# Gated scan with two MLPs: weight signs and sums on GpSimd, no plain group in the second unit, a first slot of native fp32 products

## The chip, the cores and the metric

One core of one Trainium2 chip runs the whole program. The metric is the device time of one execution in microseconds (us). The kernel before takes 1967.82 us, the median of three runs (1967.82 to 1968.0).

## The reference, cut to what matters

```python
sig = 1 / (1 + exp(-f_logit));  f = lb + (1 - lb) * sig;  i = 1 - f
h = 0
for t in range(6080):                # 2 batches, 256 features
    h = f[:, t] * h + i[:, t] * x[:, t];  y[:, t] = h
x1 = square(max(y @ w_in1, 0)) @ w_out1          # 12160 tokens, 256 -> 2048 -> 256
h2 = x1 @ w_in2
out = where(h2 > 0, h2, exp(min(h2, 0)) - 1) @ w_out2     # 256 -> 2048 -> 256
```

All is fp32. A gated recurrence along the sequence is followed by two MLPs over 12160 tokens.

## The kernel before, in words

**Arithmetic.** TensorE multiplies fp32r operands. Each fp32 operand is split into a rounded high part (a copy with fp32r output, mostly on ScalarE) and a low part (the operand minus its high part, on VectorE). `three` (L894) forms one product by three matmuls: high·high, high·low, low·high. GpSimd takes hardly any part.

**Units and slots.** The tokens are cut into units of two halves; the first unit has halves of 512 and 384 tokens, the others of 512 and 512 (the end differs). The 2048 inner features are cut into 8 groups. The work on one group of one unit is a slot. In a *plain* slot of one half, two feature blocks k times two outputs make four products, 12 matmuls. In a *mixed* slot both halves are combined by sums and differences of operands, so that seven products (21 matmuls) stand for the eight of two plain slots (24 matmuls). Mixed slots need four sums of each weight tile (`weight_sums`, L378 to L382) and differences of the features (`minus`, L611). `plain` (L248) says which slots are plain: all of the first layer's first unit, and with `PLAIN_G = 1` also group 0 of the second unit. Then `add_mixed_parts` and `add_later_parts` make that unit's operands; a unit without plain slots is served by `add_parts`.

**Weights.** `add_weights` (L424) makes each of the 32 weight tiles once. SP loads the raw tile (`st`); ScalarE takes the scaled magnitude of the high words (L437) and converts the low words (L440); VectorE shifts and joins them (`magnitude`, L443), then sets the sign bit (`sign`, L446); ScalarE makes the high part (L474) and VectorE the low part (L480). First-layer input tiles are kept in DRAM and loaded again for later units.

**The first unit.** x and f_logit rows come in four chunks (256, 256, 256, 128 tokens). For each, TensorE transposes the rows (L739), ScalarE takes a tanh (L746, L770), a gate is formed (L795/L797; for the chunks after the first by GpSimd), VectorE multiplies (L753, L776) and scans (L818). The scan runs on features not yet multiplied by `ga = 0.5 - 0.5·lb`; `split_scaled` (L549) multiplies while it makes the high part (ScalarE, L551) and the low part (VectorE, L554). For the first half, `add_first_parts` (L558) does that per chunk and feature block, four pairs in all. `products_of` (L1042) issues the first slot as two sets of 12 matmuls of 256 columns. Spins (L716) are transposes of a constant ahead of the real work.

**Order.** TensorE's order of products is written out by `pe_order`, with due times. All other steps are given to `Order`, a planner with a cost, a due time, reads and writes for each step; it decides the order on each engine, and for some steps between ScalarE and VectorE. Each engine then runs its list in order. SP issues nearly all DMAs: rows, weights, copies kept in DRAM, reloads, spills, results. `EARLY` and `WDUE` place the first weight loads and weight steps, `LOADS` names the first-unit slots before which the second unit's row loads may not start, `FIRST_DUE` the first split parts.

Of the kernel before, what the change touches and what calls it, by code (L numbers as in the profile page):

```python
# [11 lines left out]
U32 = mybir.dt.uint32  # L12
AF = mybir.ActivationFunctionType
# [3 lines left out]
P = 128  # L17
# [4 lines left out]
PLAIN_G = 1  # L22
# [4 lines left out]
GAP = 56  # L27
TURN = 0.125
# [3 lines left out]
EARLY = (-18.5,)  # L32
DUE1 = 3.0
FIRST_SLOTS = True
SPIN = (11, 16, 5)
C_DUE = 1.0
# [4 lines left out]
WDUE = (-6.0, -4.0, -2.0, 0.0)  # L41
FIRST_DUE = (-10.0, -6.0)
# [7 lines left out]
LOADS = (6, 8, 10, 12)  # L50
# [20 lines left out]
class Order:  # L71
# [47 lines left out]
    def run(self):  # L119
# [33 lines left out]
        while any(ready.values()):  # L153
            best = None
            for e, r in ready.items():
                if not r:
                    continue
                t0 = max(free[e], min(r.values()))
                n = min((n for n, t in r.items() if t <= t0 + self.HOLD), key=lambda n: steps[n][2])
                if t0 < self.RAMP:  # L160
                    late = t0 > self.CALM
                    v = min((n for n, t in r.items() if t <= t0 + self.WAIT[late]), key=lambda n: steps[n][2])
                    if steps[v][2] < steps[n][2] - self.FAR[late]:
# [28 lines left out]
def kernel(  # L192
# [67 lines left out]
    def slots_of(m, u):  # L260

        if not plain(m, u):
            return [(m, u, None, g) for g in range(KG)]
        a, b = ([(m, u, h, g) for g in range(KG) if plain(m, u, g)] for h in range(2))
        if u == 0 and FIRST_SLOTS:
            got, a, b = [*a[:3], *b[:1]], a[3:], b[1:]
            return got + [s for pair in zip(b, a) for s in pair] + b[-2:]
# [110 lines left out]
    def weight_sums(q, a):  # L378
        nc.vector.tensor_tensor(q[:, 0], a[:, 0], a[:, 2], op=ALU.add)
        nc.vector.tensor_tensor(q[:, 2], a[:, 1], a[:, 0], op=ALU.subtract)  # L380
        nc.vector.tensor_tensor(q[:, 1], q[:, 0], a[:, 1], op=ALU.subtract)
        nc.vector.tensor_tensor(q[:, 3], a[:, 3], q[:, 1], op=ALU.subtract)  # L382
# [41 lines left out]
    def add_weights(i, m, kind, c, due, wk=None):  # L424
# [22 lines left out]

        def sums(e):
# [53 lines left out]
        w = wk if kind == 0 else ("w", m, c)  # L502
        over = [("raw", k) for k in range(KG) if m == kind == 1]
# [3 lines left out]
            ["DVE", dve(CE), low_part, [a], [w]],  # L507
# [4 lines left out]
    def add_sums(c, due):  # L512
# [8 lines left out]
        chain(due - 4.0, [["DVE", 4 * dve(P), sums, [("raw", c)], [q]]])  # L521
# [12 lines left out]

    F_t = {}
# [22 lines left out]
    def add_first_parts(F, k, src, dst, due):  # L558

        x_k[0, 0, 0] = [(*k, q, c, p) for q in range(2) for c in range(KD) for p in range(2)]  # L560
        for q, (at, n) in enumerate(chunks(0, 0)):
            for c in range(KD):
                high, low = split_scaled(c, lambda at=at, n=n, c=c: src()[:, c, at : at + n], lambda at=at, n=n, c=c: dst()[:, :, c, at : at + n])
                hi, lo = (*k, q, c, 0), (*k, q, c, 1)
                order.add("ACT", act(n), due + FIRST_DUE[q] - 1.0 + C_DUE * c, high, [(*F[q], c)] + [(*k, 0, 0, 0)] * (q + c > 0), [hi])
                order.add("DVE", dve(n), due + FIRST_DUE[q] + C_DUE * c, low, [hi, (*F[q], c)], [lo])

# [152 lines left out]
    def add_scan(i, u, h, q, due, after=None, from_=None):  # L720
# [58 lines left out]
        def load_bound(e):  # L779
            nc.scalar.dma_start(lb, lower_bound.rearrange("(i c) -> i c", c=KD))  # L780

# [17 lines left out]

        def bound(e):  # L800
            nc.vector.tensor_scalar(ga, lb, -0.5, 0.5, op0=ALU.mult, op1=ALU.add)
            nc.vector.tensor_scalar(gb, lb, 0.5, 0.5, op0=ALU.mult, op1=ALU.add)
# [36 lines left out]
        if u == 0:  # L839
# [5 lines left out]
            if i == 0:  # L845
                order.add("ACT", 0.6, -30.0, load_bound, (), [("lb",)], None, 1)
            if i == 0:
                add_spin(SPIN[0], due - 7.0)
            if i == 0 and BY_TILE:
# [5 lines left out]
                order.add("DVE", 0.2, -2.0, bound, [("lb",)], [("bound",)])  # L855
# [10 lines left out]
            if i == 1:  # L866
# [3 lines left out]
                *([["DVE", 0.2, bound, [("lb",)], [("bound",)]]] if i == 0 else []),  # L870
                *(["POOL", 0.05 + n / 256, gate(c), [("bound",), fT] + [(*gT, 0)] * c, [(*gT, c)]] for c in range(KD)),
# [145 lines left out]
    def add_plain(s, wk):  # L1017
# [24 lines left out]
        def products_of(q):  # L1042
            def go(e):
                at, m = chunks(u, h)[q]
                for w, k, c in PLAIN_PRODUCTS:
# [3 lines left out]
                    three(t[c][:, cols], ws_t[wk], w, x_t[0, u, h][:, :, :, cols], k, k == 0, k == 1, True)  # L1049
# [200 lines left out]

    weights = []
# [21 lines left out]
    for due, what, m, g, who in weights:  # L1273
# [12 lines left out]
        else:  # L1286
            add_weights(n_prep, m, int(what == "out"), g, due + WDUE[min(n_prep, len(WDUE) - 1)], wk)
# [85 lines left out]
```

## Time and profile before

| | us |
|---|---|
| median of three runs | 1967.82 |
| time of the profiled execution | 1967.67 |
| its span | 1965.9 |
| TensorE busy (matmul) | 1957.9 |
| VectorE busy | 1504.6 |
| ScalarE busy | 1624.9 |
| GpSimd busy | 7.9 (12 instructions) |

The profiled execution lies 0.15 us below the median, and 1.8 us of its time lie outside the span. The granted clock is full over the whole span. Busy shares are means over stages that have different limits: the start, the first unit (about 80 us), the long middle, and the end.

### The profile page before, as it was taken

Reading aid. Unit: us, or ns where it says so; the run is one execution under the profiler, and the core shown is the slowest. Engines: PE = TensorE matmul, PEld = TensorE weight load, DVE = VectorE, ACT = ScalarE, POOL = GpSimd, SP = SyncE. Lnnn points to the kernel's source line nnn. Section 1 sums busy time; section 2 is a strip of 40 time slices with the busy share of each in tenths; the row PEclk is TensorE's granted clock in tenths of the full one; section 3 lists DMA queues with packets and bytes.
Section 4 is the critical chain, followed back from the end, with each engine's and each line's share of the span. In section 5 each row is a group of like instructions: output and inputs, shape, how many; then the busy total and the mean of one; then the engine's idle time right before and its main releaser. Section 6 shows DMA issues by size and latency. Waiting matters only on the chain.

```text
span 1965.9 us, 23805 instructions
## 1 busy us (share of the span) xinstructions
PE 1957.9 (100%) x8739; PEld 1634.4 (83%) x8739; DVE 1504.6 (77%) x1938; ACT 1624.9 (83%) x2184; POOL 7.9 (0%) x12
## 2 busy tenths in 40 slices
PE   9999999999999999999999999999999999999999
PEld 8888888888888888888888888888888888888888
DVE  8998889877776876877777687687775668778686
ACT  8989899888788878888878887887887878878786
POOL 1000000000000000000000000000000000000000
PEclk9999999999999999999999999999999999999999
DMA  7775565532533433354243343324323324242332
GB/s 255 222 234 191 193 190 191 179 128 85 147 126 115 130 106 134 105 148 137 86 137 136 105 137 115 122 101 127 136 94 107 122 99 137 94 136 97 114 116 74
DMA packets 226564, 265.80 MB, mean 135 GB/s; under 512 B 151696, under 2 KB 154256, under 8 KB 226448
## 3 DMA queue, kind: packets, MB, share of 16 engines
q1 hardware_dynamic: 224448, 263.83, 41.6%
q8 instruction: 68, 1.11, 0.2%
q10 hardware_dynamic: 2000, 0.46, 0.1%
q14 instruction: 48, 0.39, 0.1%
HBM read 222.56 MB, written 41.68 MB: 134 GB/s over the span
## 4 chain that ended last, share of the span: by engine, by line
PE 99%; DVE 1%; ACT 0%; issue 0%; POOL 0%; DVEq 0%; POOLq 0%
PE a L1181 53%; PE c L896 46%; DVE F L818 0%; PE a L716 0%; DVE wo L443 0%; PE c L739 0%; DVE wo L446 0%; DVE xT L776 0%; DVE o L1220 0%; DVE F L480 0%; ACT st L440 0%; DVE ws L480 0%; ACT wo L437 0%; ACT xa L551 0%; DVE xT L753 0%
## 5 line engine op out<-in xcount | busy, mean ns | idle before, releaser
L1181 PE MATMUL a<-g,wo 128*128 128x512 f32 (+2 forms) x4608 | 1156.3, 387 | 0.0
L1181 PEld LDWEIGHTS a<-g,wo 128*128 128x128 f32 x4608 | 863.8, 188 | 171.3
L1117 ACT ACTIVATE r<-c 128x512 f32<-128x512 f32 (+1 forms) x732 | 427.1, 583 | 252.6 <-PE c L896 246.1
L944 DVE TENSOR_TENSOR g<-r,g 128x1024 fp32r<-128x1024 f32 (+2 forms) x382 | 461.6, 1208 | 139.8 <-ACT g L939 131.4
L1124 DVE TENSOR_TENSOR r<-c,r 128x512 f32<-128x512 f32 (+1 forms) x549 | 375.5, 684 | 193.4 <-PE c L896 189.7
L939 ACT ACTIVATE g<-r 128x1024 fp32r<-128x1024 f32 (+2 forms) x382 | 401.7, 1052 | 68.5 <-PE a L1181 51.8
L896 PE MATMUL c<-xa,ws 128*128 128x512 f32 (+2 forms) x1719 | 446.2, 387 | 1.0 <-DVE ws L480 0.9
L896 PEld LDWEIGHTS c<-xa,ws 128*128 128x128 f32 x1719 | 321.2, 188 | 65.7 <-DVE ws L480 1.1
L896 PE MATMUL c<-xb,ws 128*128 128x512 f32 (+2 forms) x1152 | 318.0, 386 | 0.0
L934 DVE SCALAR_TENSOR_TENSOR r<-e,r 128x1024 f32<-128x1024 f32 (+1 forms) x190 | 230.7, 1214 | 105.0 <-ACT e L931 105.0
L896 PE MATMUL c<-xc,ws 128*128 128x512 f32 (+1 forms) x1104 | 308.9, 388 | 0.0
L896 PEld LDWEIGHTS c<-xb,ws 128*128 128x128 f32 x1152 | 215.7, 188 | 42.2
L896 PEld LDWEIGHTS c<-xc,ws 128*128 128x128 f32 x1104 | 207.1, 188 | 42.1
L931 ACT ACTIVATE e<-e 128x1024 f32<-128x1024 f32 (+1 forms) x190 | 198.8, 1046 | 0.7
L928 ACT ACTIVATE e<-r 128x1024 f32<-128x1024 f32 (+1 forms) x190 | 197.0, 1041 | 0.4
L922 ACT ACTIVATE r<-r 128x1024 f32<-128x1024 f32 (+1 forms) x186 | 194.1, 1044 | 0.2
L915 ACT ACTIVATE r<-r 128x1024 f32<-128x1024 f32 x87 | 91.2, 1048 | 0.0
L614 DVE TENSOR_TENSOR F<-F 128x512 f32<-128x512 f32 (+1 forms) x92 | 62.8, 683 | 1.0
L918 ACT ACTIVATE r<-r 128x512 f32<-128x512 f32 x87 | 53.7, 617 | 0.0
L818 DVE TENSOR_TENSOR_SCAN F<-fT,F,xT 128x256 f32<-128x256 f32 x66 | 48.2, 742 | 0.7
L545 DVE TENSOR_TENSOR xa<-F,xa 128x512 fp32r<-128x512 f32 (+3 forms) x47 | 43.6, 932 | 0.4
L1220 DVE STREAM_TRANSPOSE o<-a 128x512 f32<-128x512 f32 (+1 forms) x48 | 31.2, 686 | 1.2 <-PE a L1181 1.2
(89 smaller groups left out, 621.6 us busy)
## 6 DMA issues: line engine op xcount, KB each, us to landing
ws<-wd SPq DMA_DIRECT2D x183, 896.0 KB, 4.8
xd<-o SPq DMA_DIRECT2D x46, 256.0 KB, 2.9
fs<-in_f_logit_dram SPq DMA_DIRECT2D x176, 64.0 KB, 2.3
xs<-in_x_dram SPq DMA_DIRECT2D x176, 64.0 KB, 2.5
F<-xd SPq DMA_DIRECT2D x22, 512.0 KB, 4.4
out_dram<-o SPq DMA_DIRECT2D x88, 128.0 KB, 5.3
st<-in_moe_w_in_dram SPq DMA_DIRECT2D x16, 512.0 KB, 4.6
st<-in_moe_w_out_dram SPq DMA_DIRECT2D x16, 512.0 KB, 4.7
```

The costliest lines, as they stand in the source:

```text
L614: nc.vector.tensor_tensor(f[:, to], f[:, i], f[:, k], op=ALU.subtract)
L896: nc.tensor.matmul(out, lhsT=ws[:, p, w], rhs=xs[:, r, v], start=start and q == 0, stop=stop and q == 2, skip_group_check=check,)
L915: nc.scalar.activation(r_t[0], r_t[0], AF.Relu)
L922: nc.scalar.activation(r_t[0], r_t[0], AF.Square)
L928: nc.scalar.activation(t["e"], r_t[0], AF.Relu, scale=-1.0)
L931: nc.scalar.activation(t["e"], t["e"], AF.Exp, scale=-1.0)
L934: nc.vector.scalar_tensor_tensor(r_t[0], t["e"], 1.0, r_t[0], op0=ALU.subtract, op1=ALU.max)
L939: nc.scalar.activation(g_t[s, which][:, 0], r_t[0], AF.Copy)
L944: nc.vector.tensor_tensor(g_t[s, which][:, 1], r_t[0], g_t[s, which][:, 0].bitcast(F32), op=ALU.subtract)
L1117: nc.scalar.activation(r[0][:, i], t[A], f)
L1124: nc.vector.tensor_tensor(r[:, i], t[tag], r[:, i], op=ALU.add)
L1181: nc.tensor.matmul(a, lhsT=y, rhs=v, start=begin and jj == 0 and p == 0, stop=end and jj == len(mine) - 1 and p == 2, skip_group_check=True,)
```

## The change

- `weight_sums` is issued on GpSimd in place of VectorE.
- For weight tiles from the fifth on (`BYTES = 4`), VectorE's `sign` is left out. GpSimd writes a byte of 0 or 128 (`sign_byte`) into the top byte of the converted low word, between the conversion and `magnitude`, which then joins the sign too.
- `PLAIN_G = 0`: the second unit has only mixed slots and uses `add_parts`.
- The first slot multiplies unsplit features by `first["w"]`, the first tile times `ga` (ScalarE, `times_ga`), with native fp32 matmuls: 8 of 256 columns for 24 fp32r ones. The first tile's split comes `W_LATER` later, its low part on GpSimd. The first half's features are split over all 512 tokens at once, two pairs in place of four.
- The second chunk's gate for feature block 0 goes from GpSimd to VectorE or ScalarE.
- The second weight tile's load is put early on SP (`EARLY`), due times of the second and third tile move, the second unit's row loads may start after slots 2, 4, 6, 8, and the planner's holding rules differ before 22 us of its own clock. Load and use of the lower bound move in the source, with the same due times.

```diff
-PLAIN_G = 1
+PLAIN_G = 0
+UNTIL = 22.0
+HOLD0 = 0.1
+FAR0 = 5.0
+BYTES = 4
+SIGN_US = 1.8
-EARLY = (-18.5,)
+EARLY = (-18.5, -16.5)
-WDUE = (-6.0, -4.0, -2.0, 0.0)
-FIRST_DUE = (-10.0, -6.0)
+WDUE = (-6.0, -7.0, -5.0, 0.0)
+ADUE = -2.0
+W_LATER = 6.0
+RAW_MM = 1.78
-LOADS = (6, 8, 10, 12)
+LOADS = (2, 4, 6, 8)
...
     def weight_sums(q, a):
-        nc.vector.tensor_tensor(q[:, 0], a[:, 0], a[:, 2], op=ALU.add)
+        nc.gpsimd.tensor_tensor(q[:, 0], a[:, 0], a[:, 2], op=ALU.add)
...
+        def sign_byte(e):
+            b = t["st"].bitcast(U8).rearrange("p k e w -> p (k e) w")[:, :, 3]
+            nc.gpsimd.tensor_scalar(b, t["high"].bitcast(F32), 0.0, 128.0, op0=ALU.is_lt, op1=ALU.mult)
...
         def low_part(e):
             for v, hi, lo in parts():
-                nc.vector.tensor_tensor(lo, v, hi.bitcast(F32), op=ALU.subtract)
+                (nc.gpsimd if e == "POOL" else nc.vector).tensor_tensor(lo, v, hi.bitcast(F32), op=ALU.subtract)
...
+        if i >= BYTES:
+            steps[3:] = [["POOL", SIGN_US, sign_byte, [], [st]], ["DVE", dve(CE), magnitude, [st], [a]]]
...
-            chain(due - 6.0, [*steps, ["DVE", 4 * dve(P), sums, [a], [q]]])
+            chain(due - 6.0, [*steps, ["POOL", 2.5, sums, [a], [q]]])
...
+        if i == 0:
+            def times_ga(e):
+                first["w"] = new("a", [P, 4, P])
+                for k in range(KD):
+                    nc.scalar.activation(first["w"][:, 2 * k : 2 * k + 2], t["a"][:, 2 * k : 2 * k + 2], AF.Copy, scale=ga[:, k : k + 1])
+
+            first["key"] = key_of("a")
+            chain(due, [*steps, ["ACT", act(CE) + 0.1, times_ga, [a, ("bound",)], [first["key"]]]])
+            steps = []
+            due += W_LATER
...
-            ["DVE", dve(CE), low_part, [a], [w]],
+            ["POOL", 2.0, low_part, [a], [w]] if i == 0 else ["DVE", dve(CE), low_part, [a], [w]],
...
-        chain(due - 4.0, [["DVE", 4 * dve(P), sums, [("raw", c)], [q]]])
+        chain(due - 4.0, [["POOL", 2.5, sums, [("raw", c)], [q]]])
...
-        x_k[0, 0, 0] = [(*k, q, c, p) for q in range(2) for c in range(KD) for p in range(2)]
-        for q, (at, n) in enumerate(chunks(0, 0)):
-            for c in range(KD):
...
+        n = units[0][0]
+        x_k[0, 0, 0] = [(*k, c, p) for c in range(KD) for p in range(2)]
+        for c in range(KD):
+            high, low = split_scaled(c, lambda c=c: src()[:, c], lambda c=c: dst()[:, :, c])
...
-                *(["POOL", 0.05 + n / 256, gate(c), [("bound",), fT] + [(*gT, 0)] * c, [(*gT, c)]] for c in range(KD)),
+                *(["POOL", 0.05 + n / 256, gate(c), [("bound",), fT] + [(*gT, 0)] * c, [(*gT, c)]] if i > 1 or c else ["DVE", dve(n) + 0.08, gate(c), [("bound",), fT], [(*gT, c)], ("ACT", act(n) + 0.24)] for c in range(KD)),
...
-                    three(t[c][:, cols], ws_t[wk], w, x_t[0, u, h][:, :, :, cols], k, k == 0, k == 1, True)
+                    nc.tensor.matmul(
+                        t[c][:, cols], lhsT=first["w"][:, w], rhs=F_t[0, u][:, h + 2 * k, cols],
+                        start=k == 0, stop=k == 1, skip_group_check=True,
+                    )
...
-                x_k1 = x_k[m, u, h][4 * q : 4 * q + 4]
-                n1 = order.add("PE", COLD[q] * 6 * ROW * n, in_due[s] + 6 * q * ROW * n, products_of(q), [*x_k1, wk], [ck[0], ck[1], ("pe",)])
+                x_k1 = [("F0", u, h, q, c) for c in range(KD)]
+                n1 = order.add("PE", RAW_MM, in_due[s] + 6 * q * ROW * n, products_of(q), [*x_k1, first["key"]], [ck[0], ck[1], ("pe",)])
```

## Rows read from the trace of the kernel before

**Rows 1.** The page, busy time by engine: busy us, share, instructions.
```profile
PE 1957.9 (100%) x8739; PEld 1634.4 (83%) x8739; DVE 1504.6 (77%) x1938; ACT 1624.9 (83%) x2184; POOL 7.9 (0%) x12
```

**Rows 2.** Waits of TensorE, first 60 us: total us, times, longest.
```profile
PE c L896 <- DVE ws L480: 0.9, 1, 0.9
PE c L896 <- DVE F L480: 0.5, 1, 0.5
```

**Rows 3.** The chain that ended last, first 32 us: start, us, what.
```profile
7.56 0.57 ACT wo L437
...
9.74 0.68 DVE wo L446
...
17.06 0.59 DVE F L480
...
17.70 9.48 PE c L896 x46
```

**Rows 4.** Windows: length, then busy us of PE, PEld, DVE, ACT, POOL.
```profile
60.00:80.00 20.00, 20.00 (x104) 18.26 (x103) 19.93 (x34) 19.30 (x33) 0.00 (x0) 1.00 0.76 206
...
1900.00:1966.00 66.00, 61.25 (x303) 56.43 (x301) 42.30 (x53) 45.44 (x69) 0.00 (x0) 1.00 0.32 95
```

**Rows 5.** Timeline of TensorE, start and unit boundary: start, us, instructions, wait before them.
```profile
11.14 0.51 PE L896 MATMUL c<-xa,ws 128*128 128x256 f32 x2
...
14.98 1.67 PE L896 MATMUL c<-xa,ws 128*128 128x256 f32 x12
...
17.70 2.56 PE L896 MATMUL c<-xa,F 128*128 128x512 f32 x10 [0.45 <-DVE F L480]
20.10 2.88 PE L896 MATMUL c<-xa,ws 128*128 128x512 f32 x12
22.82 2.27 PE L896 MATMUL c<-xb,ws 128*128 128x384 f32 x12
...
82.92 2.88 PE L896 MATMUL c<-xa,ws 128*128 128x512 f32 x12
...
95.11 0.86 PE L896 MATMUL c<-xa,ws 128*128 128x512 f32 x3
```

**Rows 6.** Groups by form, VectorE: count, busy us, mean ns, idle before.
```profile
L797 DVE TENSOR_SCALAR fT<-fT,ga,gb 128x256 f32<-128x256 f32 x83 | 31.4, 404 | 0.9
...
L446 DVE SCALAR_TENSOR_TENSOR a<-st,a 128x512 int32<-128x512 int32 x24 | 16.2, 681 | 0.1
...
L480 DVE TENSOR_TENSOR ws<-wo,ws 128x512 fp32r<-128x512 f32 x4 | 2.7, 680 | 0.0
...
L379 DVE TENSOR_TENSOR a<-wo 128x128 f32<-128x128 f32 x8 | 2.3, 282 | 0.0
...
L554 DVE SCALAR_TENSOR_TENSOR xa<-F,ga,xa 128x256 fp32r<-128x256 f32 x4 | 2.0, 492 | 0.0
...
L554 DVE SCALAR_TENSOR_TENSOR xb<-F,ga,xb 128x384 fp32r<-128x384 f32 x2 | 1.2, 600 | 0.0
```

**Rows 7.** Timeline of GpSimd: all its gates.
```profile
9.69 1.61 POOL L797 TENSOR_SCALAR e<-fT,ga,gb 128x256 f32<-128x256 f32 x2 [8.39 <-ACT fT L770]
11.67 2.35 POOL L797 TENSOR_SCALAR e<-fT,ga,gb 128x256 f32<-128x256 f32 x2 [0.37 <-ACT fT L770]
15.88 3.23 POOL L797 TENSOR_SCALAR e<-fT,ga,gb 128x128 f32<-128x128 f32 x2 [1.85 <-ACT fT L770]
```

**Rows 8.** Timeline of VectorE beside the last of these.
```profile
16.32 0.74 DVE L818 TENSOR_TENSOR_SCAN F<-e,F,xT 128x256 f32<-128x256 f32 x1
...
17.57 0.77 DVE L446 SCALAR_TENSOR_TENSOR wo<-st,wo 128x512 int32<-128x512 int32 x1
```

**Rows 9.** Timeline of SP and ScalarE: early weight loads, second unit's rows.
```profile
6.12 1.21 SPq L376 DMA_DIRECT2D st<-in_moe_w_in_dram  x2
...
12.71 0.69 ACT L437 ACTIVATE wo<-st 128x512 f32<-128x512 f32 x1 [0.28 <-DMA st<-in_moe_w_in_dram]
...
34.71 1.90 SPq L761 DMA_DIRECT2D fs<-in_f_logit_dram  x4
```

More of the change, by code (lines that the diff above doesn't have):

```diff
@@ L12 @@
 U32 = mybir.dt.uint32
+U8 = mybir.dt.uint8
 AF = mybir.ActivationFunctionType
@@ L31 @@
 COLD = (1.06, 1.06)
-EARLY = (-18.5,)
+EARLY = (-18.5, -16.5)
 DUE1 = 3.0
 FIRST_SLOTS = True
+FIRST_A = (3, 1)
 SPIN = (11, 16, 5)
-C_DUE = 1.0
 BY_TILE = True
@@ L158, in run @@
                 t0 = max(free[e], min(r.values()))
-                n = min((n for n, t in r.items() if t <= t0 + self.HOLD), key=lambda n: steps[n][2])
+                n = min((n for n, t in r.items() if t <= t0 + (HOLD0 if t0 < UNTIL else self.HOLD)), key=lambda n: steps[n][2])
                 if t0 < self.RAMP:
@@ L162, in run @@
                     v = min((n for n, t in r.items() if t <= t0 + self.WAIT[late]), key=lambda n: steps[n][2])
-                    if steps[v][2] < steps[n][2] - self.FAR[late]:
+                    if steps[v][2] < steps[n][2] - (FAR0 if t0 < UNTIL else self.FAR[late]):
                         n = v
@@ L265, in slots_of @@
         if u == 0 and FIRST_SLOTS:
-            got, a, b = [*a[:3], *b[:1]], a[3:], b[1:]
-            return got + [s for pair in zip(b, a) for s in pair] + b[-2:]
+            k, j = FIRST_A
+            got, a, b = [*a[:k], *b[:j]], a[k:], b[j:]
+            return got + [s for pair in zip(b, a) for s in pair] + b[len(a) :]
         got = a[:LEAD]
@@ L378, in weight_sums @@
     def weight_sums(q, a):
[L379 to L382 removed]
+        nc.gpsimd.tensor_tensor(q[:, 0], a[:, 0], a[:, 2], op=ALU.add)
+        nc.gpsimd.tensor_tensor(q[:, 2], a[:, 1], a[:, 0], op=ALU.subtract)
+        nc.gpsimd.tensor_tensor(q[:, 1], q[:, 0], a[:, 1], op=ALU.subtract)
+        nc.gpsimd.tensor_tensor(q[:, 3], a[:, 3], q[:, 1], op=ALU.subtract)
     def plain_weights(key):
@@ L533, in add_stream @@
         order.add("SP", 0.5, due - 8.0, load, [("wd", m, c, 0)] + [("wd", m, c, 4)] * (not plain(m, u, c)), [wk], None, 512 if plain(m, u, c) else 917)
+    first = {}
     F_t = {}
@@ L558, in add_first_parts @@
     def add_first_parts(F, k, src, dst, due):
-        x_k[0, 0, 0] = [(*k, q, c, p) for q in range(2) for c in range(KD) for p in range(2)]
-        for q, (at, n) in enumerate(chunks(0, 0)):
-            for c in range(KD):
[L563 to L566, printed above, removed]
+        n = units[0][0]
+        x_k[0, 0, 0] = [(*k, c, p) for c in range(KD) for p in range(2)]
+        for c in range(KD):
+            high, low = split_scaled(c, lambda c=c: src()[:, c], lambda c=c: dst()[:, :, c])
+            f = [(*v, c) for v in F]
+            order.add("ACT", act(n), due + ADUE - 1.0 + c, high, f + [(*k, 0, 0)] * c, [(*k, c, 0)])
+            order.add("DVE", dve(n), due + ADUE + c, low, [(*k, c, 0), *f], [(*k, c, 1)])
     def add_plain_parts(u, h, F):
@@ L845, in add_scan @@
             if i == 0:
-                order.add("ACT", 0.6, -30.0, load_bound, (), [("lb",)], None, 1)
-            if i == 0:
                 add_spin(SPIN[0], due - 7.0)
@@ L854, in add_scan @@
                 add_spin(SPIN[1], due - 5.0)
-                order.add("DVE", 0.2, -2.0, bound, [("lb",)], [("bound",)])
                 for c in range(KD):
@@ L1249, in add_reload, with load_bound, bound @@
         return [F[0]], [F[1]], [F[0]], [F[1]]
+    def load_bound(e):
+        nc.scalar.dma_start(lb, lower_bound.rearrange("(i c) -> i c", c=KD))
+    def bound(e):
+        nc.vector.tensor_scalar(ga, lb, -0.5, 0.5, op0=ALU.mult, op1=ALU.add)
+        nc.vector.tensor_scalar(gb, lb, 0.5, 0.5, op0=ALU.mult, op1=ALU.add)
+    order.add("ACT", 0.6, -30.0, load_bound, (), [("lb",)], None, 1)
+    order.add("DVE", 0.2, -2.0, bound, [("lb",)], [("bound",)])
     weights = []
@@ L1286 @@
         else:
-            add_weights(n_prep, m, int(what == "out"), g, due + WDUE[min(n_prep, len(WDUE) - 1)], wk)
+            add_weights(n_prep, m, int(what == "out"), g, due + (WDUE[n_prep] if n_prep < len(WDUE) else 0.0), wk)
             n_prep += 1
```

6 lines of the change are left out of this document (removed).

## The prediction

> **What bounds the kernel now.** I read the page's busy times first. TensorE is busy for 1957.9 of 1965.9 us [rows 1], so only two things can change the time by much: the work that TensorE is given, and the few microseconds in which it waits. The waits of TensorE say where those are: 0.9 us for the low part of the first weight tile and 0.5 us for that of the second, both in the first 18 us [rows 2]. Behind that no wait is listed, and the windows show TensorE full until the last one, whose 66 us have 61.25 us of it [rows 4]; the rest there is the evacuation and store of the result, which the change doesn't touch.
>
> The chain that ended last tells what holds the start. From 7.56 us, where ScalarE takes up the first weight tile, to the end of the second tile's low part at 17.66 us it goes over ScalarE and VectorE steps; from 17.70 us it is TensorE alone [rows 3]. So a first microsecond saved by VectorE before 17.7 us is a microsecond of the end, if nothing behind it runs late. That "if" matters: between 60 and 80 us VectorE is busy for 19.93 of 20 us and ScalarE for 19.30 [rows 4]. The first unit has two engines at their limit beside TensorE, and they are only just in time.
>
> **The change part by part.** The sum is made against the profiled execution, 1967.67 us, which is 0.15 us below the median of the runs.
>
> *Group 0 of the second unit.* 24 matmuls of 512 columns become 21. Twelve of them take from 20.10 to 22.82 us, 0.227 us each [rows 5]. Three fewer: **-0.68 us**, in a stretch in which TensorE has no other limit. The output products stay 24.
>
> *The first slot's matmuls.* 24 fp32r matmuls of 256 columns go; twelve took 1.67 us, 0.139 each [rows 5], 3.34 us in all. Eight native fp32 ones come, and no row shows such a one. Below, each takes 0.139 us like a single matmul of its width (1.1 us in all); above, it takes four of these, 0.556 us (4.45 us in all), since a full product of two operands in two parts has four partial products. The rows nearest to it are the three matmuls that each replaces, 0.417 us together, and the planner's entry in the diff is 1.78 us for four, 0.445 each. I take 0.445: 3.56 us, **+0.2 us** of TensorE time, with -2.2 and +1.1 as ends. TensorE waits in this stretch, so the sum below uses this only to see when the second slot could start.
>
> The Trainium skill (FP8 and Floating Point Precision, TensorE Precision Notes) gives true fp32 four passes through the array. By that, with 0.139 us a pass, the slot would take 4.45 us, 0.9 more than I take; no row here shows it.
>
> *What must be ready for the second slot.* In the kernel before, 2 of its 12 matmuls are done by 17.70 us, so without the wait it would have run as from 17.25 us. Before that time VectorE loses: four low parts of the features at 0.492 us; two of 512 columns come. From 0.492 at 256 and 0.600 at 384 columns I extend to 0.71 at 512 [rows 6], so 1.97 becomes 1.42, -0.55 us. The first tile's low part, 0.68 us [rows 6], goes to GpSimd: it is next wanted by the second half's first slot at 22.82 us [rows 5], hidden behind two slots; if GpSimd took over 6 us for it, it would be late there. One gate comes to VectorE at 0.40 us (or goes to ScalarE). Together -0.83 us.
>
> A second saving is order. The second tile's load is issued at 6.12 us and lands at 12.7, where ScalarE waits for it [rows 9]. It moves ahead of the third chunk's two row loads on SP. That is one DMA of 512 KB moved past two of 256 KB, so it should land some 2 us earlier and the third chunk's rows 1 to 2 us later; those rows feed a scan for 22.82 us, and that slack is the cover. Then VectorE can finish the second tile before it does work that is wanted only later. In the kernel before three such steps stand ahead of 17 us, a multiplication, the third tile's magnitude and a scan, some 2.1 us by the 0.68 and 0.74 of [rows 6, 8]. They aren't saved, only deferred, and the slots behind are then short by as much.
>
> On ScalarE, `times_ga` (two copies of half a tile) comes in place of the high part, a few tenths longer; the per-chunk feature copy that stood just ahead of 7.56 us goes away. I set these against each other at nothing: the first product then starts about where it does now, at 11.14 us [rows 5]. From there 3.56 us of native products let the second slot start at 14.9 at the earliest; by VectorE's 0.83 us alone it starts at 16.4. I take 16.0, nearer to the second since what is deferred comes due at once: **-1.25 us**, with 0 and -2.35 as ends.
>
> *Signs.* For 12 tiles of the first unit VectorE loses 0.68 us each [rows 6], 8.2 us in all (16 more tiles come later). *Sums:* four steps of 0.28 us each [rows 6] for 16 tiles, 18 us in all, some three tiles of it in the first unit. All this is beside TensorE and gives 0 by itself; what it buys is air on VectorE, which the start's deferred steps and the earlier operands of the second unit use up.
>
> *Second unit.* Its first mixed slot starts where the first plain one does now, at 82.92 us; the first product that wants differences, now at 95.11 us [rows 5], moves about 9 us ahead. VectorE must do these some 5 us of differences and splits earlier, and the second half's scans with them. The 11.6 us freed by signs and sums before that pay for it; without them it would stall TensorE by several microseconds. On SP the row loads (four pairs of four DMAs, the first now at 34.71 us, 1.90 us of SP for four [rows 9]) may go before the tile loads and kept copies that they follow now. The planner's due times keep tiles first; I cost it at nothing, and at up to 3.8 us once if a pair stands before a tile that is wanted. Group 0's reload is larger for a mixed slot and has the spare buffer as cover. The bound's load and use keep their due times: nothing.
>
> The sum: 1967.67 - 0.68 - 1.25 = 1965.74, and with the 0.15 us to the median **1965.8**; 0.2 of the native products is inside the 1.25.
>
> **The rivals.** *The start gives nothing.* Native products near 0.556 us, or VectorE filling what it saved with the steps that were deferred, leave TensorE dense from the same time on. This is also the case where the new parts don't do what they are for. Only 0.68 us remains: 1967.1. For it: VectorE is full from 9 us on. Against: the chain's VectorE steps do get fewer.
>
> *The start gives all.* TensorE is dense from the first product, second slot at 14.9 us: 1967.67 - 0.68 - 2.35 + 0.15 = 1964.8, and 1964.2 if the first product starts 0.6 us earlier as the feature copy ahead of it goes.
>
> *GpSimd's signs come late (slower).* Place: each tile from the fifth on, where VectorE's in-order queue waits at `magnitude` for a GpSimd step, and behind it stand the low parts that TensorE wants. Price: the gates took 0.80 us at 256 columns with VectorE less full and 1.62 at 128 with it full [rows 7], 3.1 to 12.6 ns a column. A sign of 512 columns thus takes 1.6 to 6.5 us. I take the planner's 1.8, near the 256-column rows; their mean over all six gates would give 2.9. VectorE gains 0.68 us per tile, so up to 2.5 us nothing is lost; at 2.9 it is 12 x 0.4 = 5 us, 1970.9, and more for longer ones.
>
> *VectorE is shut out while GpSimd works.* At the fastest row a sign holds 1.6 us and a sum step 0.4 us: 12 signs and some 12 sum steps are 24 us, against 11.6 us freed, in a stretch with 0.07 us idle in 20. That gives up to +12 us, 1978. Against it: the steps of VectorE beside the slowest gates took 0.74 and 0.77 us [rows 8], where the free sign takes 0.68 [rows 6]; it is GpSimd that grew longer. The Trainium skill (SBUF — State Buffer, Who interferes with whom) has the rule behind this rival: an instruction of VectorE with two SBUF inputs and one of GpSimd that reads SBUF exclude each other, and the second to issue stands still. The trace agrees for GpSimd alone: VectorE's 0.74 and 0.77 us [rows 8] bear out little of it.
>
> **How the numbers follow.** Forecast 0.52, start gives nothing 0.20, gives all 0.12, late signs 0.11, VectorE shut out 0.05. About 0.2%, 3.9 us, is what a measurement of this kernel can tell from no change; that puts the bounds at 1963.9 and 1971.8. Below lies only the far end of "gives all": 0.03. Above lie most of the late signs and of the shutting out, 0.11 by my reckoning. Between: 0.86. The range, 1964.2 to 1970.0 us, takes in both ends of the start and short lateness of signs, and leaves out some 0.17, nearly all of it above. The likeliest case alone is 1965.0 to 1966.6.
>
> **What would show it.** Right: TensorE's matmul count falls by 19 (16 in the first slot, 3 in the second unit); eight matmuls of 256 columns follow each other at about 0.44 us; the second slot starts near 16 us and TensorE is listed with no wait behind 20 us; VectorE's busy time falls by some 35 us and GpSimd's rises by 60 to 150. Wrong: a wait of TensorE for low parts between 20 and 100 us, VectorE waiting at L443 for GpSimd for over 0.7 us a tile, or VectorE steps longer than their rows here.

## The result and the profile after

The kernel after takes 1982.95 us, the median of six runs (1981.06 to 1984.1), against 1967.82 (1967.48 to 1968.0) for the kernel before beside it. The ratio is 1.0076, with a 95% interval of 1.0063 to 1.0089: slower by 15 us, and outside the predicted range. The profiled execution of after took 1981.06 us, 1.9 below its median; its span is 1979.2 us, 13.3 longer than before. Of all runs below one is left out of its kernel's median: one of seven of the kernel with unneeded GpSimd steps took 3317.26 us, at a granted clock of 0.556.

The page's busy times by engine answer to [rows 1]:

```profile
PE 1963.9 (99%) x8728; PEld 1633.6 (83%) x8728; DVE 1493.7 (75%) x1846; ACT 1624.0 (82%) x2181; POOL 132.6 (7%) x104
```

GpSimd took up 125 us of work. VectorE has 92 steps fewer (28 signs, 64 sums), by the lengths of [rows 6] some 37 us, but its busy time fell by only 10.9 us. In the records each step overlaps the next by some 0.08 us, so these 92 hold VectorE for nearer 30 us than 37. The rest of the gap is six further `r` steps on VectorE (6.4 us by their lengths) and steps that became longer.

The waits in the first 130 us (total us, times, longest) answer to [rows 2], where TensorE's waits for VectorE were two, both before 18 us:

```profile
ACT wo L487 <- DVE a L452: 9.0, 6, 3.0
...
ACT F L487 <- DVE wo L452: 3.2, 2, 2.8
...
PE c L911 <- ACT r L1135: 2.9, 1, 2.9
...
DVE wo L452 <- POOL st L459: 2.7, 2, 2.6
...
PE a L1199 <- DVE g L959: 2.3, 3, 1.4
...
DVE a L452 <- POOL st L459: 1.2, 1, 1.2
```

Put together, these read as a queue passing its lateness on: VectorE waits at `magnitude` (L452) for GpSimd's sign (L459), ScalarE waits for `magnitude` to make the high part (L487), and TensorE then waits for steps that stand behind these on both engines. The windows show where it ends (us; busy us of PE, PEld, DVE, ACT, POOL with instructions; granted clock; DMA share; GB/s) and answer to [rows 4]:

```profile
24.00:60.00 36.00, 34.79 (x163) 28.71 (x162) 31.85 (x39) 27.91 (x51) 29.42 (x16) 1.00 0.72 206
60.00:80.00 20.00, 19.06 (x89) 15.62 (x88) 19.72 (x26) 17.33 (x31) 12.82 (x8) 1.00 0.74 242
...
85.00:90.00 5.00, 3.61 (x18) 2.93 (x17) 5.00 (x7) 4.94 (x9) 2.13 (x1) 1.00 0.71 220
90.00:95.00 5.00, 3.74 (x16) 2.53 (x15) 5.00 (x6) 2.72 (x4) 4.92 (x7) 1.00 0.97 229
95.00:100.00 5.00, 3.11 (x11) 2.98 (x12) 5.00 (x6) 4.10 (x7) 4.92 (x5) 0.78 0.40 153
```

From 24 to 60 us VectorE stands idle for 4.15 us, 3.9 of them waiting for three signs, while TensorE already loses 1.2; from 85 to 100 us VectorE is busy without a pause, on 19 steps where it did 33 before, and TensorE has 10.46 of 15 us. TensorE's timeline (start, us, what, idle time before and its releaser) answers to [rows 5]:

```profile
11.76 1.89 PE L1064 MATMUL c<-F,a 128*128 128x256 f32 x8
...
15.50 1.68 PE L911 MATMUL c<-xa,F 128*128 128x512 f32 x4
17.71 2.14 PE L911 MATMUL c<-xa,F 128*128 128x512 f32 x8 [0.54 <-DVE xa L580]
19.69 3.18 PE L911 MATMUL c<-xa,ws 128*128 128x512 f32 x12
...
88.09 2.81 PE L1199 MATMUL a<-g,wo 128*128 128x512 f32 x11 [1.39 <-DVE g L959]
...
96.89 0.96 PE L911 MATMUL c<-xb,ws 128*128 128x512 f32 x3 [2.94 <-ACT r L1135]
97.69 3.01 PE L1199 MATMUL a<-g,wo 128*128 128x384 f32 x9
```

The span can be accounted for. I took each interval between the starts of two matmuls and subtracted the usual one of its width. What is left is by my reckoning 2.84 us before, all of it ahead of 18 us, and 15.78 us after, spread over 10 to 110 us with 4.74 us in the nineties. That is 12.9 us; the first product comes 0.62 us later (11.76 against 11.14 [rows 5]), the native products cost 0.2, three matmuls less give back 0.68: 13.1 of the 13.3 us. Another choice of what is usual moves the two sums by up to 1 us. Part of the excess is a fallen clock: the nine 384-column matmuls at 97.69 us take 0.33 us each where 0.17 is usual, and the granted clock of that window is 0.78, that is, some of it at the lower of the two levels. Before it fell TensorE had been busy for 3.61 and 3.74 of 5 us.

Two views show why VectorE gained so little. First the groups by form (count, then busy us, mean ns, idle us before them and what ended it):

```profile
L459 POOL TENSOR_SCALAR st<-st 128x512 uint8<-128x512 f32 x28 | 82.6, 2981 | 194.0 <-ACT st L449 158.6 <-DMA wd<-a 16.2 <-DMA fs<-in_f_logit_dram 12.8
...
L389 POOL TENSOR_TENSOR a<-wo 128x128 f32<-128x128 f32 x8 | 6.9, 860 | 0.0
...
L390 POOL TENSOR_TENSOR a<-a 128x128 f32<-128x128 f32 x8 | 3.7, 462 | 0.0
```

A sign takes 2.98 us in the mean, where the planner was told 1.8, and a step of the sums 0.46 to 0.86. Then the timelines of GpSimd and VectorE:

```profile
12.45 1.28 POOL L493 TENSOR_TENSOR ws<-wo,ws 128x512 fp32r<-128x512 f32 x1 [2.27 <-ACT ws L487]
...
12.61 1.67 DVE L455 SCALAR_TENSOR_TENSOR wo<-st,wo 128x512 int32<-128x512 int32 x1
...
23.64 5.64 POOL L459 TENSOR_SCALAR st<-st 128x512 uint8<-128x512 f32 x1 [4.52 <-ACT st L449]
...
23.77 1.22 DVE L939 TENSOR_TENSOR r<-r 128x1024 f32<-128x1024 f32 x1
24.91 1.22 DVE L959 TENSOR_TENSOR g<-r,g 128x1024 fp32r<-128x1024 f32 x1
...
29.31 0.98 DVE L452 SCALAR_TENSOR_TENSOR wo<-wo,st 128x512 int32<-128x512 int32 x1 [2.58 <-POOL st L459]
...
49.58 6.21 POOL L459 TENSOR_SCALAR st<-st 128x512 uint8<-128x512 f32 x2
...
53.30 0.98 DVE L452 SCALAR_TENSOR_TENSOR a<-a,st 128x512 int32<-128x512 int32 x1 [1.23 <-POOL st L459]
...
214.84 2.70 POOL L459 TENSOR_SCALAR st<-st 128x512 uint8<-128x512 f32 x1 [7.13 <-ACT st L449]
```

Late in the run, where GpSimd has little beside it, a sign still takes 2.70 us. And VectorE's own step of 0.68 us [rows 6] took 1.67 beside GpSimd's low part and 0.98 beside its signs. Counted over 10 to 130 us, against VectorE's lengths in the kernel before: 72 steps with both inputs in SBUF that ran beside a GpSimd step are longer by 9.8 us together, 36 of the same kinds that ran beside none by nothing; eight transposes (one input, L808) beside GpSimd steps by nothing, and six other steps with one input (gates, casts, a copy) by 0.7 us together. It goes the other way too: the first sign, at 23.64 us, took 5.64 us, 2.9 more than the late one, while the long VectorE steps beside it kept their 1.22 us, and VectorE then stood 2.58 us for it. A first use of the instruction is not the reason: with signs in the second layer alone (below) the first takes 2.69 us.

### The profile page after: what moved, and what is told of

Its sections match the earlier page's. It is cut to its first block, busy times and chain, and to the rows that moved or that the text cites. A ratio compares the mean times of both kernels' runs of the same rounds, so it can differ in the third digit from the quotient of the medians.

```text
span 1979.2 us, 23833 instructions
## 1 busy us (share of the span) xinstructions
PE 1963.9 (99%) x8728; PEld 1633.6 (83%) x8728; DVE 1493.7 (75%) x1846; ACT 1624.0 (82%) x2181; POOL 132.6 (7%) x104
## 4 chain that ended last, share of the span: by engine, by line
PE 93%; DVE 2%; issue 2%; POOL 1%; ACT 1%; DMA 0%; SPq 0%; DVEq 0%; POOLq 0%; ACTq 0%
PE a L1199 50%; PE c L911 43%; POOL st L459 1%; DVE g L959 0%; DVE F L837 0%; DVE a L452 0%; DMA fs<-in_f_logit_dram 0%; DVE wo L452 0%; DMA st<-in_moe_w_in_dram 0%; DVE wo L493 0%; DVE F L640 0%; DVE xT L824 0%; ACT r L1054 0%; POOL a L388 0%; DVE xa L571 0%
## 5 line engine op out<-in xcount | busy, mean ns | idle before, releaser
L911 PE MATMUL c<-xa,ws 128*128 128x512 f32 (+1 forms) x1692 | 442.8, 388 | 0.0
L459 POOL TENSOR_SCALAR st<-st 128x512 uint8<-128x512 f32 x28 | 82.6, 2981 | 194.0 <-ACT st L449 158.6
L571 DVE TENSOR_TENSOR xa<-F,xa 128x1024 fp32r<-128x1024 f32 (+3 forms) x46 | 43.9, 960 | 0.4
```

What stands on the lines that cost most here:

```text
L459: nc.gpsimd.tensor_scalar(b, t["high"].bitcast(F32), 0.0, 128.0, op0=ALU.is_lt, op1=ALU.mult)
L911: nc.tensor.matmul(out, lhsT=ws[:, p, w], rhs=xs[:, r, v], start=start and q == 0, stop=stop and q == 2, skip_group_check=check,)
```

## Experiments

All times are medians, with the kernel before at 1967.8 us beside each. The question was first which part costs what. Theory: signs and sums on GpSimd make VectorE's work late in the first unit. Rivals: the earlier operands of the second unit are too much by themselves; the start is late.

**The start alone.** Signs, sums and the plain group as before; native first slot, early loads and due times as after.

```diff
-PLAIN_G = 0
+PLAIN_G = 1
-BYTES = 4
+BYTES = 99
...
-        nc.gpsimd.tensor_tensor(q[:, 0], a[:, 0], a[:, 2], op=ALU.add)
+        nc.vector.tensor_tensor(q[:, 0], a[:, 0], a[:, 2], op=ALU.add)
...
-            chain(due - 6.0, [*steps, ["POOL", 2.5, sums, [a], [q]]])
+            chain(due - 6.0, [*steps, ["DVE", 4 * dve(P), sums, [a], [q]]])
...
```

> Signs and sums on VectorE and one plain group in the second unit, as in the kernel before; left of the change are the native first slot, the early loads and the due times. Theory D (two separate costs: the second unit's early operands, and GpSimd's work, each hidden behind the other where both are there): VectorE's load and the due times of the second unit are the old ones, so 1967 to 1968.5 us, and the 1975 us of the kernel without GpSimd's signs and sums is all the second unit. Theory E (the native first slot or the early loads cost the time): 1972 us or more, with gaps of TensorE near the start or near 90 us.

1969.52 us, ratio 1.0009 [1.0000, 1.0018]: +1.7, where the prediction had -1.25, and between the two ranges of the expectation. TensorE's timeline of this kernel:

```profile
10.95 0.75 PE L765 MATMUL a<-one,fs 128*128 128x128 f32 x4 [0.93 <-DMA fs<-in_f_logit_dram]
...
12.22 1.89 PE L1064 MATMUL c<-F,a 128*128 128x256 f32 x8
13.95 0.39 PE L765 MATMUL a<-one,fs 128*128 128x128 f32 x2
...
17.85 2.12 PE L911 MATMUL c<-xa,F 128*128 128x512 f32 x8 [0.54 <-DVE xa L580]
19.81 3.20 PE L911 MATMUL c<-xa,ws 128*128 128x512 f32 x12
22.84 0.33 PE L911 MATMUL c<-xb,ws 128*128 128x384 f32 x1
23.52 0.80 PE L911 MATMUL c<-xb,ws 128*128 128x384 f32 x3 [0.35 <-DVE xb L580]
```

The third chunk's rows, moved behind the second tile's load, are late at transposes that stand ahead of the first product in TensorE's order. It starts at 12.22 us, 1.08 later. The slots behind it wait less than before (1.17 us of excess intervals up to 20 us, for 2.84), so the third slot still starts 0.29 earlier, 19.81 against 20.10 [rows 5]. From there on 1.52 us go in the twenties, most of them in the fourth slot for low parts that VectorE makes late, and 0.49 near 100 us: -0.29 + 1.52 + 0.49 = 1.72, which is the loss. Three kernels built on this one try to mend it: the first tile's low part back on VectorE; then also the third chunk's rows ahead of the second tile; then also the old `LOADS`.

```diff
-            ["POOL", 2.0, low_part, [a], [w]] if i == 0 else ["DVE", dve(CE), low_part, [a], [w]],
+            ["DVE", dve(CE), low_part, [a], [w]],
```

> The kernel with the start alone (1969.5 us), with the first tile's low part on VectorE. Theory F (at the start GpSimd's low part holds VectorE's sign step for 1.0 us and the next feature step for 0.3, and these hold the second slot): the sign step takes 0.68 us again and the third slot starts about 0.5 to 1 us earlier; 1968.5 to 1969.2. Theory G (VectorE has as much to do as before, the low part included): within 0.3 us of 1969.5.

```diff
-EARLY = (-18.5, -16.5)
+EARLY = (-18.5,)
```

> The one above, with the second weight tile's load back behind the third chunk's rows. Theory H (the early tile makes TensorE wait for the third chunk's rows in front of the first slot, 0.7 to 0.9 us, and the first product starts at 12.2 us where its weights were ready at 10.9): the first product starts before 11.2 us. If the second tile then lands after 12.5 us, the second slot is no earlier and the time stays within 0.5 us; if VectorE has other work meanwhile, 0.5 to 1.2 us less.

```diff
-LOADS = (2, 4, 6, 8)
+LOADS = (6, 8, 10, 12)
```

> The one above, with the second unit's row loads only after slots 6, 8, 10 and 12, as in the kernel before. If the early rows cost weight tiles their time on SP's queue: 0.3 to 1.5 us less, at or under 1967.8. If they are harmless: no difference beyond 0.3 us, or up to 1 us more as the second unit's rows then come late.

They give 1968.61 (1.0005 [0.9996, 1.0013]), 1968.61 (1.0004 [0.9996, 1.0013]) and 1968.48 us (1.0003 [0.9995, 1.0012]). The low part was worth 0.9 us: in the first of them VectorE's sign at 13.23 us takes 0.68 us again. The rest changes places. In the last of them:

```profile
10.98 1.89 PE L1064 MATMUL c<-F,a 128*128 128x256 f32 x8
...
19.59 2.91 PE L911 MATMUL c<-xa,ws 128*128 128x512 f32 x12
...
23.86 0.44 PE L911 MATMUL c<-xb,ws 128*128 128x384 f32 x1 [1.02 <-DVE xb L580]
```

The first product is on time and the third slot 0.5 us earlier than in [rows 5], but the fourth then loses 1.4 us of intervals, for the most part waiting for a low part: VectorE's deferred steps come due there. Moving the fourth tile behind them made it worse:

```diff
-WDUE = (-6.0, -7.0, -5.0, 0.0)
+WDUE = (-6.0, -7.0, -5.0, 1.5)
```

> The kernel with the native first slot, the low part on VectorE and the old loads (1968.5 us), with the fourth tile's due time 1.5 us later, which puts its second VectorE step and half of its first behind the second half's features. If what the start wins by the third slot (0.5 us) is lost at the fourth, where TensorE waits 1.3 us for features that VectorE makes after that tile: the wait falls under 0.5 us, and 1967.2 to 1967.9. If the fourth tile is then late for its output products instead: no gain, 1968.3 or more.

1970.34 us, 1.0014 [1.0005, 1.0022].

**One part at a time, on top of the start alone.** No plain group, signs on GpSimd, or sums on GpSimd:

```diff
-PLAIN_G = 1
+PLAIN_G = 0
```

> The changed kernel with signs and sums on VectorE: what is left is the first slot's native products and the second unit without a plain group. A and B: 1966 to 1968 us, a little under the kernel before, since GpSimd has little more to do than there. C: VectorE has its old load and an earlier due time for the second unit's operands, so 1971 or more, with the gaps near 90 us.

```diff
-BYTES = 99
+BYTES = 4
```

> As the one above, with the signs on GpSimd (sums on VectorE, a plain group in the second unit). Theory A/D: late signs cost by themselves, 1975 to 1983 us, with gaps of TensorE at output products between 30 and 90 us. If signs were harmless without the sums and the early operands: under 1970 us.

```diff
-        nc.vector.tensor_tensor(q[:, 0], a[:, 0], a[:, 2], op=ALU.add)
+        nc.gpsimd.tensor_tensor(q[:, 0], a[:, 0], a[:, 2], op=ALU.add)
...
-            chain(due - 6.0, [*steps, ["DVE", 4 * dve(P), sums, [a], [q]]])
+            chain(due - 6.0, [*steps, ["POOL", 2.5, sums, [a], [q]]])
...
```

> As the first of these, with the sums on GpSimd (signs on VectorE, a plain group). Theory A/D: sums aren't urgent and take 0.5 to 0.9 us a step, so within 2 us of the first of these. Theory B (sharing lengthens VectorE's steps, whoever waits): 3 to 6 us above the first of these, with VectorE's steps lengthened by some 4 us in the first 110.

And from the kernel after, one part at a time taken back: signs to VectorE, sums to VectorE, the plain group.

```diff
-BYTES = 4
+BYTES = 99
```

> The changed kernel with all signs back on VectorE (sums, first slot and the second unit as changed). Theory A (signs come late: 2.7 to 4.1 us each on GpSimd where the planner was told 1.8, and VectorE's queue waits behind them): nearly all of the 15 us comes back, 1966 to 1969 us, and no wait of VectorE for GpSimd is left in the first unit. Theory B (GpSimd's work of either kind lengthens VectorE's steps): the sums still do that, so only part comes back, 1971 to 1977. Theory C (the second unit without a plain group wants its operands too early): little comes back, above 1976.

```diff
-        nc.gpsimd.tensor_tensor(q[:, 0], a[:, 0], a[:, 2], op=ALU.add)
+        nc.vector.tensor_tensor(q[:, 0], a[:, 0], a[:, 2], op=ALU.add)
...
-            chain(due - 6.0, [*steps, ["POOL", 2.5, sums, [a], [q]]])
+            chain(due - 6.0, [*steps, ["DVE", 4 * dve(P), sums, [a], [q]]])
...
```

> The changed kernel with the sums back on VectorE, signs still on GpSimd. A: the time stays within 2 us of 1983, or rises by up to 4 since VectorE gets 1.1 us of work more for each tile. B: falls by 3 to 6 us, as the 32 steps of the first layer's sums no longer stand in VectorE's way. C: as the changed kernel or worse.

```diff
-PLAIN_G = 0
+PLAIN_G = 1
```

> The changed kernel with one plain group in the second unit again. A and B: stays above 1978 us, as late signs and longer VectorE steps are there as before. C: the gaps of TensorE between 86 and 97 us (1.6 and 3.1 us, of some 13 in all) go, 1976 to 1978 with 0.7 us more products; if C were all of it, 1970 to 1972.

| signs | sums | plain group | us | ratio [95%] |
|---|---|---|---|---|
| VectorE | VectorE | yes | 1969.52 | 1.0009 [1.0000, 1.0018] |
| VectorE | VectorE | no | 1975.07 | 1.0037 [1.0023, 1.0051] |
| VectorE | GpSimd | yes | 1972.66 | 1.0025 [1.0016, 1.0035] |
| VectorE | GpSimd | no | 1980.65 | 1.0065 [1.0049, 1.0080] |
| GpSimd | VectorE | yes | 1981.79 | 1.0072 [1.0057, 1.0087] |
| GpSimd | VectorE | no | 1978.9 | 1.0055 [1.0040, 1.0070] |
| GpSimd | GpSimd | yes | 1983.57 | 1.0079 [1.0064, 1.0094] |
| GpSimd | GpSimd | no (after) | 1982.95 | 1.0076 [1.0063, 1.0089] |

Each part costs by itself: signs +12.3, no plain group +5.6, sums +3.1. Together these are 21, but after stands only 13.4 above the start alone: stops of one part lie in the same stretch as those of another, and who removes one meets the next. So a difference between two rows is no fixed price. Moving the signs costs 2.3 to 12.3 us by the neighbours it has, the sums 1.8 to 5.6, and dropping the plain group between -2.9 and +8.0. The row without any of the three is the fastest. Each row also has its own plan: between the first and the fifth row TensorE's list is the same, VectorE's and ScalarE's are not, so a difference holds the new order as well as the new steps.

Against the expectations: taking the signs back gave 2.3 of the 15 us, the little that was expected if the second unit's early operands are the cost. Sums moved alone (+3.1) and sums taken back (-4.1) lie in the ranges set for sharing.

**No plain group in the kernel before.** A rival was that this step needs the native start or GpSimd's sharing to hurt.

```diff
-PLAIN_G = 1
+PLAIN_G = 0
```

> The kernel before with only the plain group of the second unit taken away. If the missing plain group costs by itself (VectorE has no time for the second unit's differences before they are due): 1971 to 1976 us, with gaps of TensorE near 85 to 95 us and a lower clock behind them. If it cost only together with the early loads and the other due times: 1967.0 to 1968, with 0.7 us of products saved.

1975.46 us, 1.0040 [1.0025, 1.0056]: +7.6 with no step of the weights on GpSimd and three matmuls fewer. Its windows, and its waits from 18 to 120 us:

```profile
80.00:85.00 5.00, 5.00 (x24) 4.02 (x22) 5.00 (x9) 4.30 (x8) 0.00 (x0) 1.00 0.83 223
85.00:90.00 5.00, 1.99 (x5) 0.77 (x4) 5.00 (x10) 2.51 (x4) 0.00 (x0) 0.82 0.80 200
90.00:95.00 5.00, 3.62 (x10) 3.07 (x10) 4.88 (x11) 2.87 (x5) 0.00 (x0) 0.50 0.65 247
```

```profile
PE c L896 <- DVE xb L545: 1.4, 1, 1.4
...
PE c L896 <- DVE xa L545: 1.2, 1, 1.2
PE c L896 <- ACT xa L542: 1.1, 1, 1.1
```

The first mixed slot waits for its operands part by part while VectorE is full, and behind these waits the clock falls to 0.50, the 1.2 GHz level, for what comes next. GpSimd does nothing in these windows and the start is the old one, which settles the rival.

**What it is about the signs.** Three causes were open: VectorE waits for a GpSimd step that the planner takes for shorter than it is; GpSimd's steps lengthen VectorE's; or in-order queues turn either into larger stops. The price was told first, in the kernel after (3.2 us), in the kernel with signs alone, and in after with 3.6 us for the sums as well:

```diff
-SIGN_US = 1.8
+SIGN_US = 3.2
```

> The changed kernel with the planner told 3.2 us for a sign in place of 1.8. Theory A in the form that the order is wrong because the cost is: the planner places magnitude later and other VectorE work in the gap, 1974 to 1979 us. In the form that VectorE lacks the time whatever the order, or that sharing is the cost (B): above 1979.

> The kernel with the signs alone on GpSimd (1981.8 us) with the planner told 3.2 us for a sign in place of 1.8. Theory A in the form of a wrong plan (each engine's list was made for signs of 1.8 us, so VectorE and ScalarE stand in order before steps whose inputs are late, while needed work waits behind): falls to about the 1973.9 us of the kernel with unneeded signs, 1973 to 1976. If signs on the path cost as such, whatever the plan: above 1979.

```diff
-            chain(due - 6.0, [*steps, ["POOL", 2.5, sums, [a], [q]]])
+            chain(due - 6.0, [*steps, ["POOL", 3.6, sums, [a], [q]]])
...
```

> The whole change with the planner told 3.2 us for a sign and 3.6 for four sum steps (0.9 each, as between 56 and 92 us in the changed kernel). Wrong plan: at or below the 1978.6 us of telling it the signs alone, 1975 to 1979, where some 4 us of sharing and some 5 of the missing plain group are left. Otherwise no lower than 1978.6.

1978.56 (1.0056 [1.0039, 1.0073]), 1980.28 (1.0064 [1.0051, 1.0078]) and 1981.12 us (1.0068 [1.0055, 1.0082]). The right price takes 4.4 us off the kernel after, which lies in the range set there for a wrong plan. But it takes 1.5 off the signs alone, where 6 to 9 were expected of that cause, and 1.8 where the sums are priced too. It moves the stops about, and the mis-told price is a part of the cause at most.

Next, steps like the signs whose bytes go to a spare tile that nobody reads. The operation and the shape are the sign's, but they read the low word in place of the high one and write bytes three apart, and they are 20, not the 28 of the expectation: 12 in the first unit and 8 later, since `add_weights` returns before this point for the other 8 tiles of the second layer. VectorE keeps its own signs, so this kernel adds unneeded work only:

```diff
...
+        if i >= 4:
+            def unused(e):
+                b = spare.rearrange("p (n w) -> p n w", w=3)[:, :, 0]
+                nc.gpsimd.tensor_scalar(b, t["low"].bitcast(F32), 0.0, 128.0, op0=ALU.is_lt, op1=ALU.mult)
+
+            order.add("POOL", SIGN_US, due - 4.0, unused, [st], [])
```

> The kernel with the start alone (signs and sums on VectorE), with 28 further GpSimd steps of the sign's operation on the same words, whose result goes to a spare tile and for which nothing but the next load into that buffer waits: the work of the signs without VectorE's wait and without VectorE's relief. Theory B (sharing): VectorE's steps lengthen by 4 to 8 us in the first 110 us and the time is 4 to 10 us above 1969.5. Theory A (waiting): VectorE's steps lengthen by under 2 us and the time is within 2 us of 1969.5, so that the 12 us of the signs alone are the wait.

1973.6 us (the median of six runs, 1973.08 to 1973.88), 1.0029 [1.0017, 1.0041]: +4.1 over the start alone. The lists of TensorE, VectorE, ScalarE and SP are the same, instruction for instruction, as in the start alone; no wait for these steps is listed on any of these engines, and nothing was taken from VectorE. So this is the price of running beside it. Counted as above, VectorE's steps between 10 and 130 us are 5.0 us longer than in the start alone.

Then, with real signs again, their number: 28 (the signs alone, as above), those from the eleventh tile on (22), and those of the second layer's 16 tiles alone.

```diff
-BYTES = 4
+BYTES = 10
```

> The same with the last 22 tiles, so that 6 signs of the first unit are on GpSimd in place of 12. If each sign there costs about the same (1 us a sign): 1974 to 1977. If the cost lies in a few places where ScalarE or VectorE stands in order before a late step and TensorE stops for 3 to 4 us: anything between 1969.5 and 1982, not half.

```diff
-BYTES = 4
+BYTES = 16
```

> The kernel with the signs alone on GpSimd (1981.8 us), but for the last 16 weight tiles only, which are made when the first unit is over. If what counts is the first unit, where VectorE and ScalarE have no idle time: within 0.5 us of the 1969.5 us of the kernel with the start alone. If a sign on GpSimd costs wherever it stands (0.4 us a tile on the average of 28 tiles): 1975 to 1977.

Over the start alone: 28 signs +12.3, 22 signs +5.2 (1974.73, 1.0036 [1.0022, 1.0049]), 16 signs +1.6 (1971.1, 1.0017 [1.0008, 1.0026]). Six signs in the first part of the first unit make 7 us of the 12.3. The time with 22 signs lies in the range expected of an even price as well as in that of a few stops, and 16 signs cost more than the 0.5 us and less than the 5.5 of the two expectations, so the times alone don't decide. The timelines do: with 22 signs TensorE is busy without a pause from 30 to 95 us; with 28 it loses 2.2 us in the thirties and 5.2 in the seventies. In the kernel with signs alone:

```profile
62.70 6.32 POOL L459 TENSOR_SCALAR st<-st 128x512 uint8<-128x512 f32 x2 [3.07 <-ACT st L449]
...
63.64 0.70 DVE L808 STREAM_TRANSPOSE fT<-fs 128x512 f32<-128x512 f32 x1
...
64.89 1.56 DVE L820 TENSOR_SCALAR fT<-fT,ga,gb 128x256 f32<-128x256 f32 x1
66.38 1.11 DVE L452 SCALAR_TENSOR_TENSOR wo<-wo,st 128x512 int32<-128x512 int32 x1
...
74.33 0.63 ACT L568 ACTIVATE xa<-F 128x512 fp32r<-128x512 f32 x1 [5.68 <-PE c L911]
...
77.61 0.62 ACT L487 ACTIVATE wo<-a 128x512 fp32r<-128x512 f32 x1
...
78.28 4.01 PE L1199 MATMUL a<-g,wo 128*128 128x512 f32 x10 [4.00 <-ACT wo L487]
```

Weight work falls behind; at 74 us ScalarE's next step in order is a split into `xa` that begins only when TensorE has read the old `xa`, and ScalarE stands for 5.68 us. The high part that TensorE wants next (L487) stands five steps behind it, and TensorE stands for 4.00 us. In the start alone ScalarE stands for 0.77 us at this split, and the high part that TensorE wants next is made by then. One stop of ScalarE's order alone is a third of the 12.3 us. Behind it the granted clock is 0.79 between 75 and 80 us, and the next ten matmuls take 0.40 us each where 0.227 is usual, some 1.7 us more.

What stays open: of the signs' 12.3 us, some 5.7 are shown as this stop and the clock behind it. Sharing is shown to cost 4.1 us where all lists stay as they were. With signs alone VectorE's steps are longer by about as much, 4.5 us over the start alone, but how much of that reaches TensorE there was not separated, nor what belongs to VectorE's waits at `magnitude` (3.0 us) and to other stops. And no run moves the signs while the planner's order stays, so how much is the new order is not shown.

## Why the prediction was wrong

It forecast 1965.8 us and no measurable change; 1982.95 came. By its steps:

- **Group 0 of the second unit, -0.68:** three matmuls less are there (the count fell by 11: 24 fewer, 16 more records of native products, three fewer). The gain drowned in what the step called for.
- **Native products, 3.56 us of 0.445 each:** right. Eight records for four products take 1.89 us, 0.47 each, and the next instruction of TensorE follows 1.73 us after the first of them (12.22 to 13.95 us in the start alone), 0.43 each. The estimate that the prediction made by the Trainium skill (FP8 and Floating Point Precision, TensorE Precision Notes), 4.45 us with 0.139 us for each of four passes, was too long; how many passes there are the trace does not show.
- **The second slot at 16.0, -1.25:** it started at 15.50 us but stopped, and its last eight matmuls began at 17.71, where the last ten had begun before [rows 5]; the third slot is 0.41 us earlier, for the 1.25 forecast. ("14.9 at the earliest" has 0.2 us that the prediction doesn't give: 11.14 and 3.56 make 14.70. Measured, the second slot starts 3.74 us behind the first product, the transposes between included.) Three parts of the step failed. The deferred VectorE steps, "the slots behind are then short by as much", were named and not charged: with the start alone the fourth slot loses more than the third had gained. "Those rows feed a scan for 22.82 us, and that slack is the cover" overlooked that the rows' transposes stand ahead of the first product in TensorE's order. And the first tile's low part was "hidden behind two slots" as far as its use goes, but cost VectorE 0.99 us of its next step. Even with these two undone, the rival that the start gives nothing is what the runs show (1968.48 to 1968.61, not told from the time before).
- **Signs and sums, "gives 0 by itself":** the step that failed most. The sign was taken at the planner's 1.8 us although the mean of all six gates [rows 7] had given 2.9; it measured 2.98 in the mean, 2.70 late in the run and 5.64 at the worst. The rival of late signs put 2.9 us at +5, counting 0.4 us lost a tile; it left out that steps behind in order wait too, and alone the signs cost 12.3.
- **VectorE shut out, 0.05:** too little. From 0.74 and 0.77 us [rows 8] I concluded that only GpSimd gives way. For the first sign it did; but steps with two SBUF inputs grew by up to 0.99 us, 9.8 us over the first unit and its surroundings, and 20 unneeded steps put 4.1 us on the time by this alone. The rule of the Trainium skill (SBUF — State Buffer, Who interferes with whom) held better than my reading of two rows: two-input steps were lengthened, transposes with one input were not. Of the exclusive lock that it tells of the trace shows a part: the 0.68 us step at 12.61 us ended 0.55 after GpSimd's 1.28 us step, as if it had waited for it, but most steps beside a 3 us sign lost far less than that.
- **The second unit's early operands, "the 11.6 us freed by signs and sums before that pay for it; without them it would stall TensorE by several microseconds":** the second half was right: +7.6 in the kernel before, +5.6 on the new start. The first half was wrong: between 85 and 100 us VectorE was as full as before, since in place of the steps that it lost it got the lengthening and the waits. What the sum lacked besides is the clock, which fell to 0.50 and 0.78 behind the stops.

The signs named as wrong showed: TensorE waits between 20 and 100 us, VectorE's at `magnitude` up to 2.6 us, and longer steps.

## What to carry to other kernels

Moving work off a full engine frees it only if the new engine neither makes it wait nor runs at its expense: price the moved step by the measured row most like it (not by the plan's figure), then ask who stands behind the wait in every in-order queue. Before work is made due earlier in a stretch where one engine is busy 19.93 of 20 us, try that step alone on the old kernel: here it showed +7.6 us at once. And when a load is moved up, look not at the last use of what it passes but at the first step in any engine's order that touches it.

## What was not expected of the hardware

- A GpSimd step with a comparison and a multiplication over 512 columns of fp32, writing single bytes four apart, takes 2.70 us with little beside it, and 2.98 in the mean of 28.
- Even a VectorE step with one tensor input can be held up until a sign ends: with signs alone 128x256 took 1.56 us (L820, at 64.89 us) where 0.40 is usual [rows 6], and ended 0.14 us after the first of the two signs at 62.70 us. Over the kernels with signs, ten steps of this line took 0.80 to 1.56 us and ended 0.14 or 0.15 us after a sign; others beside signs took 0.37 to 0.75. The Trainium skill (SBUF — State Buffer, Who interferes with whom) counts tensor_scalar among the steps that can take, in some modes, the pair of ports shared with GpSimd. These ten agree with that; which mode they ran in the trace does not show.
- The profile records a native fp32 matmul of 256 columns as two matmuls; 16 records stand for 8 products.
